# Pooled attention and a gated MLP on one core: left-over tokens stored token by token, two small vectors loaded late, half of a weight loaded through GpSimd's queue

## The chip, the cores and the metric

The kernel runs on one core of a Trainium2 chip. A time is the device time of one execution in microseconds (us); where several runs are given, their median counts. The engines are TensorE (PE in the profile; PEld is its weight load), VectorE (DVE), ScalarE (ACT), GpSimd (POOL) and SyncE (SP). SP computes nothing here; it issues DMAs.

## What is computed

```python
# B, H, S, D = 8, 8, 576, 64; keys and values are averaged over groups of 8 tokens: 72 of each
k_p = k.reshape(B, H, 72, 8, D).mean(axis=3);  v_p = v.reshape(B, H, 72, 8, D).mean(axis=3)
attn = softmax(q @ k_p.T / sqrt(D))              # 576 x 72 for each batch and head
x = (attn @ v_p), heads side by side             # [B, 576, 512]
h = gelu(x @ w_in)                               # w_in 512 x 1024
u, v = h[..., :512], h[..., 512:]
v_n = (v - mean) / sqrt(var + 1e-6) * g_ln       # over the 512 features
v_s = w_sg @ v_n + b_sg[:, None]                 # over the 576 tokens
out = x + (u * v_s) @ w_out
```

`w_in` and `w_out` arrive as 64-bit floats, and the kernel makes 32-bit floats of them with integer operations.

## The kernel before

**Steps and the written-out order.** The work of a batch is cut into steps named by a letter and a number: A and B load k and v, E loads the left-over tokens, C loads q, K pools the keys and writes the block matrix `kbd`, P pools the values, Q transposes q, S makes scores and softmax, L and T transpose the attention weights, V multiplies by the values (this gives x), H makes the value half of h and normalises it, U the other half, W multiplies by `w_sg` and gates, O multiplies by `w_out`, Z stores. Lower-case names are weights: `lv0`, `lv1` load the two pieces of w_in's value half, `lu0`, `lu1` those of its other half, `lo0`, `lo1` those of w_out, `ls0` loads w_sg; `v0` to `v3`, `u0` to `u3`, `o0` to `o3` and `s0` to `s4` convert or transpose one piece each. A step is a generator, and each time its name stands in a list it advances by one piece. `PROLOGUE` is that list for batch 0 and the beginning of batches 1 to 3, together with all the weights; `PERIOD` is run once for each later batch. `S0+1` is the first group of heads one batch later. Each engine issues its instructions in the order in which the lists emit them.

**Left-over tokens.** 72 pooled tokens of a head are 64, which have tiles of their own, and 8 left over. `load_left` brings the raw tokens of those 8 of all 8 heads into one tile `left`, four DMAs of 32 rows of 2 KB (lines 263 and 266): keys in partitions 96 to 127, values in 64 to 95. A row is a head and a token, and the tokens of a head stand together. The pooled rows `lp` (L315) are transposed with the pooled keys (L336, L338) and copied into `kbd` (L345, L346). The attention weights of left-over tokens are gathered by GpSimd into `el` (L465), transposed (step L), and split into `lt` (L476 or L479, L480 and L482), which step V multiplies by `vl`, the left-over values times `mask` (L381).

**Start.** GpSimd writes the constants, among them `mask` with a memset and two selects (L112 to L116). SP issues all loads, in the order of the list: all of them go through `load` (L155). In one queue at most eight of SP's DMAs are under way: the ninth waits for the first. b_sg, spread over 128 partitions as `bbc`, and g_ln as `gcol` are loaded with w_sg in `load_wsg`, and are first read in step W (L616).

**Conversion of w_in.** A piece is converted by two ACT instructions (L196, L197), two of DVE (L199, L200), one of POOL (L202), an ACT cast (L205) into `wih` and a POOL subtraction (L207) into `wil`.

**The row around the first V of batch 1.** The two halves of `lt` each need two ACT casts (L479, L480) and one DVE subtraction (L482); the last four normalised tiles of H (`vg`, L575) are cast to `vhh` or `vht` (L583), which step W multiplies.

Of the kernel before, what the change touches and what calls it, by code (L numbers as in the profile page):

```python
# [20 lines left out]


PROLOGUE = """
A1+0 A0+0 lv0 v1 E0+0 v1 K0+0 C0+0 v0 K0+0 K2+0 C1+0 K1+0 C2+0 Q0+0 K1+0 K2+0 Q1+0 v0 Q0+0 K2+0 C3+0 S0+0 v1 v0 lv1
Q2+0 v1 S0+0 B1+0 B0+0 Q3+0 Q1+0 v1 ls0 S1+0 v0 S1+0 Q2+0 S0+0 E0+1 S1+0 S0+0 S2+0 Q3+0 A0+1 v3 T0+0 S1+0 S2+0 S3+0
S0+0 v3 S3+0 S3+0 S2+0 P0+0 lu0 v0 S2+0 S3+0 v2 v3 S3+0 A1+1 P1+0 S1+0 S2+0 S3+0 P2+0 T0+0 s3 v3 T1+0 S3+0 S3+0 L0+0
s3 v3 v2 C0+1 v2 s4 s3 T1+0 K0+1 L0+0 s4 C1+1 V0+0 B0+1 v2 K2+1 lo0 T2+0 s4 s1 V0+0 s1 T2+0 u1 v2 V1+0 V1+0 V2+0 T3+0
s2 u1 V2+0 K1+1 V0+0 T3+0 K2+1 u0 lu1 K2+1 s2 s1 u1 V3+0 Q0+1 V3+0 u0 Q1+1 s2 V1+0 S0+1 S0+1 S0+1 S1+1 u1 V2+0 V1+0
V3+0 u0 S1+1 V2+0 S0+1 S1+1 u0 V0+0 H0+0 H2+0 u1 S1+1 S0+1 S0+1 H0+0 P0+1 S0+1 H2+0 S1+1 u3 s0 s0 V3+0 T0+1 H0+0 U1+0
H2+0 s0 U1+0 S1+1 H1+0 T0+1 u0 B1+1 H0+0 P1+1 C3+1 u3 P2+1 C2+1 H2+0 H0+0 S1+1 S0+1 Q2+1 u2 u2 H2+0 H0+0 Q3+1 H1+0  # L30
P2+1 T0+1 H4+0 P2+1 H4+0 u2 H4+0 S2+1 H3+0 H2+0 S3+1 S2+1 H4+0 S1+1 C1+2 S2+1 u2 u2 u3 C0+2 H1+0 H3+0 S2+1 U0+0 u3
S3+1 u3 S3+1 S2+1 H4+0 S3+1 H3+0 U0+0 P2+1 o0 H1+0 U2+0 H4+0 S3+1 S2+1 S3+1 S2+1 U3+0 S2+1 lo1 H1+0 S3+1 o1 A1+2 o1
U2+0 E0+2 H4+0 S3+1 H1+0 L0+1 H3+0 T1+1 H3+0 L0+1 H4+0 L0+1 H3+0 Q0+2 o1 U3+0 W2+0 L0+1 o1 V0+1 o1 o3 o0 T1+1 K1+2
W2+0 T1+1 o3 W3+0 T2+1 o0 o0 W3+0 o0 V0+1 o2 V1+1 o2 T2+1 o2 T2+1 W0+0 A0+2 V1+1 V2+1 o3 K0+2 o2 W2+0 V1+1 T3+1 B0+2
W1+0 K2+2 V2+1 W2+0 T3+1 W0+0 W0+0 T3+1 W3+0 o2 K2+2 K2+2 V3+1 C2+2 W0+0 W1+0 W3+0 P0+2 W1+0 W1+0 S0+2 O0+0 S0+2 V1+1
O1+0 Q2+2 V2+1 V3+1 S0+2 B1+2 A0+3 O0+0 P1+2 Q1+2 S0+2 V3+1 S1+2 O0+0 A1+3 O1+0 P2+2 o3 S1+2 S1+2 S2+2 O2+0 O1+0 S2+2
C3+2 V0+1 S2+2 Z0+0 O2+0 S1+2 o3 V3+1 Z0+0 H2+1 H2+1 Q3+2 C0+3 O2+0 Z1+0 S0+2 T0+2
""".split()
# [12 lines left out]
def tile_pooled_attn_gmlp(ctx: ExitStack, tc: tile.TileContext, q, k, v, w_in, g_ln, w_sg, b_sg, w_out, out):  # L51
    nc = tc.nc
# [170 lines left out]

# [93 lines left out]
    def step_K(b, i):  # L317
        if i < 2:
            if ("kp", b) not in st:
                st["kp", b] = per.tile([P, G, D], F32, name="kp")  # L320
# [12 lines left out]
        kp = st.pop(("kp", b))
        ps = atile()
        for a in range(2):
            nc.tensor.transpose(ps[:, 0, P * a:P * (a + 1)],  # L336
                                kp[:, 2 * a:2 * a + 2].rearrange("p h d -> p (h d)"), ident)
        nc.tensor.transpose(ps[:, 1, 0:P], lp.rearrange("p h d -> p (h d)"), ident)  # L338
# [4 lines left out]
        for h in range(2):
            r = slice(D * h, D * h + D)
            nc.scalar.mul(kbd[r, :, JL + JM * h:JL + JM * (h + 1)], main[r], c)  # L345
            nc.scalar.mul(kbd[r, :, LEFT[h]:LEFT[h] + JL], left[r], c)  # L346
# [69 lines left out]
    def step_S(b, g):  # L416
        qT = st.pop(("qT", b, g))
        flat = (mtile() if b == 0 else atile()).rearrange("p a n -> p (a n)")
        slots = []
# [9 lines left out]
        nc.vector.tensor_reduce(out=nmax, in_=every.rearrange("p s (h k) -> p s h k", h=2),  # L429
                                axis=AX.X, op=ALU.max, negate=True)  # L430
# [4 lines left out]
        mode = 2 if (b, g) in SOFTMAX else 0
        if mode == 2:

            scores = every.rearrange("p s (h k) -> p s h k", h=2)
            nc.vector.tensor_tensor(e, scores, nmax.unsqueeze(3).broadcast_to([P, NT, 2, SP]), op=ALU.add)
            yield  # L440
            nc.scalar.activation(e, e, AF.Exp)
        else:
            for i in range(NT):
                for h in range(2):
                    acc = {} if mode else {"accum_out": ssum[:, i, h:h + 1]}
                    nc.scalar.activation(e[:, i, h], slots[i][:, h], AF.Exp, bias=nmax[:, i, h:h + 1], **acc)  # L446
# [12 lines left out]
        nc.vector.tensor_tensor(e, e, rec.unsqueeze(3).broadcast_to([P, NT, 2, SP]), op=ALU.mult)  # L459
# [4 lines left out]
        for h in range(2):
            nc.gpsimd.tensor_copy(st["el", b][:, :, JL * (2 * g + h):JL * (2 * g + h + 1)],  # L465
                                  ef[:, :, LEFT[h]:LEFT[h] + JL])
# [277 lines left out]
```

## Times and profile before

| | |
|---|---|
| runs | 584.28 us median of 3 (583.62 to 584.38) |
| profiled execution | 584.24 us, of which the span of its instructions is 582.5 us |
| PE | 554.7 us busy, 95% of the span |
| PEld, DVE, ACT, POOL | 522.9, 405.6, 351.9, 222.7 us busy |
| DMA | 46.34 MB, of which 36.23 MB are read |
| granted TensorE clock | 0.991 |

Busy time is the union of an engine's recorded instructions; the matmuls' ends are modelled. "[idle before <-releaser]" behind a row is the time in which the engine had nothing running ahead of it, and what ended that time.

### The profile page before, as it was taken

The numbers are of one execution on the slowest core, as the hardware profiler recorded it, in microseconds if no ns is written. First come the engines' busy times: TensorE is split into PE (matmuls) and PEld (weight loads), VectorE is DVE, ScalarE is ACT, GpSimd is POOL, SyncE is SP. The second block draws the span as 40 slices with busy tenths as digits, with TensorE's granted clock in tenths as the row PEclk, the third lists the DMA queues.
The fourth block names the chain that finished last, engine by engine and source line by source line (L and its number), as shares of the span: only waits on it lengthen the run. The fifth ranks groups of instructions, "written<-read, shape, count | busy, mean of one in ns | idle before, by whom it ended". The sixth has DMA issues, their size and how long they took to land.

```text
span 582.5 us, 10319 instructions
## 1 busy us (share of the span) xinstructions
PE 554.7 (95%) x3793; PEld 522.9 (90%) x3793; DVE 405.6 (70%) x555; ACT 351.9 (60%) x1000; POOL 222.7 (38%) x301
## 2 busy tenths in 40 slices
PE   3698988999999999999999999999999999999995
PEld 3576788998999989999999989999999989998995
DVE  0579998988668795778667785688667765344434
ACT  2888776788547775497456765497456775412310
POOL 4365565833326131522416231532417131433230
PEclk9899998999999999999999999999999999999998
DMA  8988460462431634233441724134350211021105
GB/s 199 240 223 236 72 169 27 100 132 47 90 73 37 117 58 97 58 68 51 94 79 37 119 56 96 33 73 72 82 90 1 43 20 21 1 42 22 20 1 82
DMA packets 161282, 46.34 MB, mean 80 GB/s; under 512 B 148752, under 2 KB 148752, under 8 KB 161232
## 3 DMA queue, kind: packets, MB, share of 16 engines
q1 hardware_dynamic: 156464, 45.10, 37.9%
q10 hardware_dynamic: 4768, 0.59, 0.7%
q8 instruction: 30, 0.49, 0.4%
q14 instruction: 20, 0.16, 0.1%
HBM read 36.23 MB, written 9.44 MB: 78 GB/s over the span
## 4 chain that ended last, share of the span: by engine, by line
PE 79%; DVE 10%; ACT 4%; DMA 3%; SPq 2%; issue 1%; ACTq 0%; POOL 0%; DVEq 0%
PE mps L99 65%; PE aps L99 11%; PE aps L135 3%; ACT e L446 2%; SPq L155 2%; DMA left<-in_v 1%; DMA qraw<-in_q 1%; DVE e L459 1%; DVE bst L569 1%; DVE nmax L429 1%; DVE vg L575 1%; DVE vp L315 1%; DMA out<-y 1%; DVE ssum L449 1%; DVE qT L412 1%
## 5 line engine op out<-in xcount | busy, mean ns | idle before, releaser
L99 PE MATMUL mps<-xhl,wih 128*128 128x288 f32 x512 | 89.9, 298 | 0.0
L627 POOL TENSOR_TENSOR glo<-u,ghi 128x576 fp32r<-128x576 f32 x32 | 45.4, 1431 | 108.7 <-ACT ghi L625 106.8
L99 PE MATMUL mps<-wih,xhl 128*128 128x512 f32 x256 | 85.6, 400 | 0.1
L99 PEld LDWEIGHTS mps<-xhl,wih 128*128 128x128 f32 x512 | 75.8, 189 | 1.4
L446 ACT ACTIVATE e<-aps,nmax 128x72 f32<-128x72 f32 x240 | 73.4, 352 | 2.7 <-DVE nmax L429 2.4
L616 DVE SCALAR_TENSOR_TENSOR mps<-mps,gcol,bbc 128x576 f32<-128x576 f32 x32 | 26.4, 826 | 51.8 <-PE mps L99 51.7
L99 PEld LDWEIGHTS mps<-wih,xhl 128*128 128x128 f32 x256 | 48.1, 188 | 10.7 <-DVE x L659 0.3
L446 ACT ACTIVATION_READ_ACCUMULATOR e<-aps,nmax 128x1 f32 x240 | 57.1, 238 | 0.0
L99 PE MATMUL mps<-wsh,vhh 128*128 128x288 f32 x256 | 56.4, 302 | 0.0
L99 PE MATMUL mps<-wsl,vhh 128*128 128x288 f32 x256 | 55.4, 298 | 0.0
L99 PE MATMUL mps<-wsh,vhl 128*128 128x288 f32 x256 | 55.2, 297 | 0.0
L99 PE MATMUL mps<-xhl,wil 128*128 128x288 f32 x256 | 55.0, 296 | 0.0
L572 POOL TENSOR_TENSOR rstd<-mv,eps 128x1 f32<-128x1 f32 (+1 forms) x40 | 11.1, 277 | 114.0 <-DVE mv L570 104.5
L527 POOL TENSOR_TENSOR xhl<-x,xhl 128x576 fp32r<-128x576 f32 x32 | 45.3, 1430 | 23.9 <-ACT xhl L525 23.9
L575 DVE TENSOR_SCALAR vg<-vg,mv,rstd 128x512 f32<-128x512 f32 (+1 forms) x40 | 40.1, 1005 | 19.3 <-POOL rstd L573 19.3
L99 PE MATMUL mps<-ghi,woh 128*128 128x288 f32 x240 | 52.7, 301 | 0.0
L99 PE MATMUL mps<-ghi,wol 128*128 128x288 f32 x240 | 51.4, 295 | 0.0
L99 PE MATMUL mps<-glo,woh 128*128 128x288 f32 x240 | 51.4, 295 | 0.0
L99 PE MATMUL mps<-wil,xhl 128*128 128x512 f32 x128 | 50.6, 395 | 0.0
L565 ACT ACTIVATE vg<-mps 128x512 f32<-128x512 f32 x32 | 19.2, 599 | 45.4 <-PE mps L99 45.2
L585 POOL TENSOR_TENSOR vhl<-vg,vhh 128x512 fp32r<-128x512 f32 x32 | 42.2, 1319 | 9.4 <-ACT vhh L583 8.7
L625 ACT CAST ghi<-u 128x576 fp32r<-128x576 f32 x32 | 21.4, 673 | 39.5 <-DVE u L618 38.8
(158 smaller groups left out, 1423.9 us busy)
## 6 DMA issues: line engine op xcount, KB each, us to landing
out<-y SPq DMA_DIRECT2D x118, 72.0 KB
kvraw<-in_k SPq DMA_DIRECT2D x32, 256.0 KB
qraw<-in_q SPq DMA_DIRECT2D x112, 72.0 KB
kvraw<-in_v SPq DMA_DIRECT2D x28, 256.0 KB
raw<-in_moe_w_in SPq DMA_DIRECT2D x4, 1024.0 KB
raw<-in_moe_w_out SPq DMA_DIRECT2D x2, 1024.0 KB
stage<-in_moe_w_sg SPq DMA_DIRECT2D x4, 288.0 KB
left<-in_k SPq DMA_DIRECT2D x16, 64.0 KB
```

The lines of the kernel that those rows point to most:

```text
L99: nc.tensor.matmul(o, lhsT, rhs, start=start, stop=stop)
L135: nc.tensor.transpose(ps[:rows, i * P:(i + 1) * P], src(i), ident if i < NT - 1 else swap)
L155: queue.dma_start(o, i)
L446: nc.scalar.activation(e[:, i, h], slots[i][:, h], AF.Exp, bias=nmax[:, i, h:h + 1], **acc)
L527: (nc.vector if b in LO_DVE else nc.gpsimd).tensor_tensor(xhl[:, 1, g], x32[:, g], xhl[:, 0, g].bitcast(F32), op=ALU.subtract)
L565: nc.scalar.activation(vg, o, AF.Gelu_apprx_tanh)
L572: nc.gpsimd.tensor_tensor(rstd, mv[:, 1:2], eps[:n, 1:2], op=ALU.add)
L575: nc.vector.tensor_scalar(vg, vg, mv[:, 0:1], rstd, op0=ALU.subtract, op1=ALU.mult)
L585: (nc.gpsimd if i < NT - 1 else nc.vector).tensor_tensor(lo, vg, hi.bitcast(F32), op=ALU.subtract)
L616: nc.vector.scalar_tensor_tensor(vs, vs, gcol[:, d:d + 1], bbc.rearrange("p (a n) -> p a n", a=2), op0=ALU.mult, op1=ALU.add)
L625: nc.scalar.copy(ghi[:, d], uf)
L627: nc.gpsimd.tensor_tensor(glo[:, d], uf, ghi[:, d].bitcast(F32), op=ALU.subtract)
```

## The change

1. `load_left` orders the rows by token first and head second (`h j g (r d)` for k, `j h (r d)` for v). What reads the rows follows: `kbd`'s copy (`p (j g)`), the place that `el` is gathered to, now with a step of four elements between the tokens, and `mask`, which is now 1/8 where the row's index modulo 4 is the column.
2. `mask` is made by DVE from the identity, by one reduction and one multiplication, instead of by GpSimd.
3. b_sg and g_ln leave `load_wsg` and have a function and a name of their own, `lb0`, late in the prologue.
4. `W_POOL = ("v",)`: the two DMAs of w_in's value half are issued by GpSimd.
5. `PROLOGUE` is written in another order. It holds the same names as before, each as often, and `lb0`. `PERIOD` is as before.

```diff
-A1+0 A0+0 lv0 v1 E0+0 v1 K0+0 C0+0 v0 K0+0 K2+0 C1+0 K1+0 C2+0 Q0+0 K1+0 K2+0 Q1+0 v0 Q0+0 K2+0 C3+0 S0+0 v1 v0 lv1
+A0+0 A1+0 E0+0 C0+0 C1+0 lv0 K0+0 K2+0 K1+0 B0+0 Q0+0 Q0+0 K0+0 C2+0 K1+0 C3+0 Q1+0 lv1 K2+0 B1+0 Q1+0 ls0 A0+1 K2+0
...
-    W_POOL = ()
+    W_POOL = ("v",)
...
-    nc.gpsimd.memset(mask, 1.0 / POOL)
     sl = mask[64:96, :]
-    nc.gpsimd.affine_select(out=sl, in_=sl, compare_op=ALU.is_ge, fill=0.0, base=0,
-                            pattern=[[-JL, 4]], channel_multiplier=1)
-    nc.gpsimd.affine_select(out=sl, in_=sl, compare_op=ALU.is_ge, fill=0.0, base=JL - 1,
-                            pattern=[[JL, 4]], channel_multiplier=-1)
+    nc.vector.tensor_reduce(out=sl, in_=ident[64:96, 64:96].rearrange("p (j a) -> p a j", a=4), axis=AX.X, op=ALU.add)
+    nc.vector.tensor_scalar(sl, sl, 1.0 / POOL, None, op0=ALU.mult)
...
+
+    def load_vectors():
         load(bbc, b_sg.rearrange("(o t) -> o t", o=1).broadcast_to([P, S]))
         load(gcol, g_ln.rearrange("(c p) -> p c", p=P))
...
-        src = k[b].rearrange("(g h) (j r) d -> h g j (r d)", h=2, r=POOL)
+        src = k[b].rearrange("(g h) (j r) d -> h j g (r d)", h=2, r=POOL)
         for h in range(2):
-            load(t[96:P, h], src[h, :, JM:SP])
-        src = v[b].rearrange("h (j r) d -> h j (r d)", r=POOL)
+            load(t[96:P, h], src[h, JM:SP])
+        src = v[b].rearrange("h (j r) d -> j h (r d)", r=POOL)
         for gp in range(2):
-            load(t[64:96, gp], src[4 * gp:4 * gp + 4, JM:SP])
+            load(t[64:96, gp], src[JM:SP, 4 * gp:4 * gp + 4])
...
-        left = ps[:, 1, 96:P].rearrange("p (g j) -> p g j", g=G)
+        left = ps[:, 1, 96:P].rearrange("p (j g) -> p g j", g=G)
...
-            nc.gpsimd.tensor_copy(st["el", b][:, :, JL * (2 * g + h):JL * (2 * g + h + 1)],
+            nc.gpsimd.tensor_copy(st["el", b].rearrange("p t (n j a) -> p t n j a", n=2, a=4)[:, :, g // 2, :, 2 * (g % 2) + h],
                                   ef[:, :, LEFT[h]:LEFT[h] + JL])
...
+            elif name[1] == "b":
+                load_vectors()
```

How the new list moves instructions shows best at three places. The first is SP's beginning, before the change: k of batch 0, the first piece of w_in's value half, the left-over tokens, then q (`early` and `qraw` are both tiles of q; `early<-in_v` is v).

```order
L155 DMA kvraw<-in_k 64x2x512 x4
L155 DMA raw<-in_moe_w_in 128x2x1024
L155 DMA left<-in_k 32x1x512 x2
L155 DMA left<-in_v 32x1x512 x2
L155 DMA early<-in_q 96x6x64 x6
L155 DMA qraw<-in_q 96x6x64 x2
L155 DMA raw<-in_moe_w_in 128x2x1024
L155 DMA early<-in_v 64x2x512 x4
L155 DMA stage<-in_moe_w_sg 128x576 x4
L155 DMA stage<-in_moe_w_sg 64x576
L155 DMA bbc<-in_moe_b_sg 128x576
L155 DMA gcol<-in_moe_g_ln 128x4x1
```

SP's beginning after the change:

```order
L152 DMA kvraw<-in_k 64x2x512 x4
L152 DMA left<-in_k 32x1x512 x2
L152 DMA left<-in_v 32x1x512 x2
L152 DMA early<-in_q 96x6x64 x4
L152 DMA early<-in_v 64x2x512 x2
L152 DMA early<-in_q 96x6x64 x2
L152 DMA qraw<-in_q 96x6x64 x2
L152 DMA early<-in_v 64x2x512 x2
L152 DMA stage<-in_moe_w_sg 128x576 x4
L152 DMA stage<-in_moe_w_sg 64x576
L152 DMA kvraw<-in_k 64x2x512 x2
L152 DMA raw<-in_moe_w_in 128x4x512
```

Both pieces of w_in's value half and the two small vectors have left this stretch; k of batch 1 follows w_sg directly, where the vectors, the left-over tokens of batch 1 and then k stood. The two pieces are now issued by GpSimd, behind its last memset and ahead of its first conversion:

```order
L350 MEMSET vb 128x512
L352 MEMSET vl 64x512
L355 MEMSET lt 64x576 x2
L152 DMA raw<-in_moe_w_in 128x2x1024 x2
L199 TENSOR_TENSOR top<-top,raw 128x512 x2
L204 TENSOR_TENSOR wil<-top,wih 128x512 x2
```

The second place is ACT's beginning, before:

```order
L196 ACT_TABLE_LOAD
L196 ACTIVATE top<-raw 128x512
L197 ACTIVATE raw<-raw 128x512
L196 ACTIVATE top<-raw 128x512
L197 ACTIVATE raw<-raw 128x512
L326 COPY kp<-aps 128x128 x2
L408 COPY qT<-mps 128x576
L345 ACTIVATE kbd<-aps 64x4x64
L346 ACTIVATE kbd<-aps 64x4x8
L345 ACTIVATE kbd<-aps 64x4x64
L346 ACTIVATE kbd<-aps 64x4x8
L205 CAST wih<-top 128x512
```

ACT's beginning after:

```order
L407 COPY qT<-mps 128x576
L325 COPY kp<-aps 128x128 x2
L407 COPY qT<-mps 128x576
L344 ACTIVATE kbd<-aps 64x4x64
L345 ACTIVATE kbd<-aps 64x4x8
L344 ACTIVATE kbd<-aps 64x4x64
L345 ACTIVATE kbd<-aps 64x4x8
L193 ACTIVATE top<-raw 128x512
L194 ACTIVATE raw<-raw 128x512
L193 ACTIVATE top<-raw 128x512
L194 ACTIVATE raw<-raw 128x512
L445 ACTIVATE e,ssum<-mps,nmax 128x72 x10
```

The first two conversions of w_in (four instructions) stood ahead of everything else and now stand between `kbd` and the first exponentials, and the second copy of q (`qT`) stands ahead of `kbd`. On PE, likewise, both first groups of q are now transposed ahead of the pooled keys. The third place is DVE ahead of the first V of batch 1, before:

```order
L459 TENSOR_TENSOR e<-e,aps 128x720
L199 TENSOR_SCALAR top<-top 128x512
L200 SCALAR_TENSOR_TENSOR top<-raw,top 128x512
L575 TENSOR_SCALAR vg<-vg,mv,rstd 128x512
L585 TENSOR_TENSOR vht<-vg,vht 64x512
L482 TENSOR_TENSOR lt<-aps,lt 32x576
L412 STREAM_TRANSPOSE qT<-qraw 128x576
L482 TENSOR_TENSOR lt<-aps,lt 32x576
```

The same stretch of DVE after:

```order
L458 TENSOR_TENSOR e<-e,aps 128x720
L574 TENSOR_SCALAR vg<-vg,mv,rstd 64x512
L196 TENSOR_SCALAR top<-top 128x512
L197 SCALAR_TENSOR_TENSOR top<-raw,top 128x512
L574 TENSOR_SCALAR vg<-vg,mv,rstd 128x512
L196 TENSOR_SCALAR top<-top 128x512
L197 SCALAR_TENSOR_TENSOR top<-raw,top 128x512
L481 TENSOR_TENSOR lt<-aps,lt 32x576
L584 TENSOR_TENSOR vht<-vg,vht 64x512
L481 TENSOR_TENSOR lt<-aps,lt 32x576
```

The 64-row `vg` has come down into this stretch, a second conversion pair stands ahead of the first `lt`, `vht` has moved between the two `lt`, and the transpose of q has moved behind them. On ACT the two casts for the first `lt` now stand ahead of the last cast of `vhh` instead of behind it.

More of the change, by code (lines that the diff above doesn't have):

```diff
@@ L23 @@
 PROLOGUE = """
-A1+0 A0+0 lv0 v1 E0+0 v1 K0+0 C0+0 v0 K0+0 K2+0 C1+0 K1+0 C2+0 Q0+0 K1+0 K2+0 Q1+0 v0 Q0+0 K2+0 C3+0 S0+0 v1 v0 lv1
[L25 to L37, printed above, removed]
+A0+0 A1+0 E0+0 C0+0 C1+0 lv0 K0+0 K2+0 K1+0 B0+0 Q0+0 Q0+0 K0+0 C2+0 K1+0 C3+0 Q1+0 lv1 K2+0 B1+0 Q1+0 ls0 A0+1 K2+0
@@ new lines @@
+v0 lu0 S0+0 S1+0 S0+0 Q2+0 Q3+0 v0 v1 S0+0 v1 v1 S1+0 Q2+0 v1 S0+0 E0+1 v0 S1+0 v0 C1+1 v1 A1+1 Q3+0 S1+0 v0 v3 S2+0
+S2+0 S1+0 T0+0 S3+0 v3 S2+0 S3+0 S0+0 v3 P1+0 S3+0 S3+0 v2 S2+0 S2+0 T0+0 v3 S3+0 S3+0 P0+0 S3+0 P2+0 C0+1 S3+0 s3
+T1+0 v3 T1+0 s4 s3 K0+1 v2 L0+0 lo0 L0+0 V0+0 s4 s4 V0+0 u1 s3 K2+1 T2+0 V1+0 T2+0 s1 u1 T3+0 K1+1 v2 V1+0 B0+1 V2+0
+v2 Q0+1 T3+0 s2 v2 Q1+1 s1 V2+0 K2+1 V3+0 K2+1 V0+0 S0+1 u0 V3+0 s1 u0 S0+1 S0+1 s2 u1 S1+1 S1+1 u1 S0+1 s2 V1+0 C3+1
+S1+1 V3+0 V2+0 u0 V0+0 S0+1 S0+1 Q3+1 V2+0 S1+1 C2+1 lu1 S0+1 H2+0 H2+0 H0+0 S1+1 T0+1 V1+0 s0 P0+1 B1+1 u1 H0+0 lb0
@@ new lines @@
+s0 T0+1 A0+2 S1+1 U1+0 s0 H2+0 u0 H0+0 u3 u0 T0+1 U1+0 H2+0 H2+0 S1+1 Q2+1 H1+0 V3+0 S0+1 u3 P1+1 S3+1 S3+1 u2 H4+0
+H1+0 H0+0 S1+1 H2+0 u3 u3 P2+1 P2+1 u2 H4+0 H0+0 P2+1 H0+0 u2 H4+0 H3+0 S3+1 S2+1 H4+0 H1+0 S2+1 H3+0 S3+1 S2+1 H1+0
+C0+2 U0+0 u3 H3+0 S2+1 S3+1 U3+0 lo1 S2+1 u2 U0+0 u2 A1+2 S2+1 H4+0 S3+1 H1+0 H1+0 P2+1 S2+1 S3+1 o0 S2+1 U3+0 H4+0
+o1 H4+0 S3+1 U2+0 C1+2 L0+1 o1 T1+1 L0+1 H3+0 H3+0 o0 L0+1 H4+0 H3+0 o1 W2+0 L0+1 U2+0 V0+1 K1+2 T1+1 o0 o0 Q1+2 o0
+o1 V0+1 W3+0 o2 T1+1 V1+1 T2+1 T2+1 o1 K0+2 W2+0 W0+0 B1+2 o2 T2+1 E0+2 Q0+2 V1+1 o2 V2+1 o3 T3+1 o3 o2 W3+0 V1+1
@@ L38 @@
+T3+1 V2+1 W0+0 K2+2 o3 W0+0 W1+0 W2+0 W0+0 T3+1 K2+2 W3+0 C2+2 o2 V3+1 K2+2 S0+2 W1+0 P1+2 V3+1 W1+0 W2+0 B0+2 S1+2
+S0+2 W1+0 S0+2 P0+2 o3 W3+0 P2+2 O1+0 O1+0 o3 Q2+2 S0+2 S0+2 A1+3 O0+0 C3+2 V0+1 O1+0 S1+2 V3+1 O0+0 S2+2 O0+0 S2+2
+O2+0 V2+1 Q3+2 S1+2 Z0+0 O2+0 O2+0 S2+2 A0+3 Z0+0 Z1+0 C0+3 H2+1 S1+2 V1+1 H2+1 V3+1 T0+2
 """.split()
```

## The prediction

> **What bounds the kernel now.** I read the page first: PE is busy nearly all the span.
>
> ```profile
> span 582.5 us, 10319 instructions
> ```
>
> The share of busy time says nothing of where the rest is lost, so next I read the busy time of each engine by stretches of the span. The columns are the stretch and its length, then busy us and count for PE, PEld, DVE, ACT and POOL, the granted clock, the DMA share and GB/s.
>
> ```profile
> 0.00:10.00 10.00, 1.82 (x8) 1.85 (x9) 0.00 (x0) 1.28 (x1) 5.93 (x24) 1.00 0.75 215
> 10.00:20.00 10.00, 8.03 (x63) 7.43 (x62) 4.93 (x6) 6.27 (x15) 3.72 (x3) 1.00 0.94 209
> 20.00:30.00 10.00, 6.31 (x39) 5.74 (x37) 5.49 (x11) 9.32 (x52) 1.67 (x4) 0.83 1.05 249
> 30.00:40.00 10.00, 8.94 (x65) 7.51 (x64) 6.76 (x11) 9.57 (x28) 6.56 (x11) 1.00 0.80 213
> 40.00:50.00 10.00, 8.75 (x44) 6.35 (x43) 9.70 (x9) 8.45 (x17) 6.46 (x5) 1.00 0.87 176
> 100.00:120.00 20.00, 20.00 (x152) 19.70 (x152) 18.67 (x20) 14.77 (x42) 15.77 (x12) 1.00 0.44 100
> ```
>
> From 100 us PE is busy 20.00 us of 20.00: there it sets the pace, and whatever arrives there earlier or later moves the end by as much. Up to 40 us the DMA share is 0.75 to 1.05, and from 20 us ACT is busy over 9 of 10. From 40 us DVE is (9.70 of 10). So the prologue is limited by transfers, then ACT, then DVE, and the change can pay only there. The chain of waits names where DVE hands over to PE, and the waits of DVE between 40 and 140 us say where that chain has slack:
>
> ```profile
> 93.50 1.68 PE aps L99 x8
> DVE kp L315 <- DMA kvraw<-in_k: 2.7, 1, 2.7
> DVE lt L482 <- ACT lt L480: 1.7, 2, 1.1
> ```
>
> At 93.50 PE starts V of batch 1, and from there it hardly waits. Ahead of it DVE waits once 2.7 us for k of batch 1 and twice, 1.7 us together, for `lt`. When that V starts is what I forecast; the rest of the program follows it.
>
> **The start, up to the last softmax of batch 0.** The DMA issues, with KB each:
>
> ```profile
> kvraw<-in_k SPq DMA_DIRECT2D x32, 256.0 KB
> raw<-in_moe_w_in SPq DMA_DIRECT2D x4, 1024.0 KB
> left<-in_k SPq DMA_DIRECT2D x16, 64.0 KB
> left<-in_v SPq DMA_DIRECT2D x16, 64.0 KB
> early<-in_q SPq DMA_DIRECT2D x6, 144.0 KB
> bbc<-in_moe_b_sg SPq DMA_DIRECT2D x1, 288.0 KB
> ```
>
> And the rows of the timeline on the way to the first scores and through ACT's stretch:
>
> ```profile
> 8.18 5.77 PE L99 MATMUL aps<-kvraw,ident 128*128 128x128 f32 x32 [8.18 <-DMA kvraw<-in_k]
> 11.92 0.67 ACT L196 ACTIVATE top<-raw 128x512 f32<-128x512 f32 x1 [9.84 <-DMA raw<-in_moe_w_in]
> 15.83 0.39 PE L336 MATMUL aps<-ident,kp 128*128 128x128 f32 x2
> 16.37 0.30 PE L338 MATMUL aps<-ident,lp 128*128 128x128 f32 x1 [0.16 <-DVE lp L315]
> 16.56 0.69 PE L405 MATMUL mps<-ident,early 96*128 96x96 f32 x6
> 16.71 0.38 ACT L345 ACTIVATE kbd<-aps 64x256 f32<-64x256 f32 x1
> 17.46 0.18 ACT L346 ACTIVATE kbd<-aps 64x32 f32<-64x32 f32 x1
> 19.78 0.64 ACT L408 COPY qT<-aps 128x576 f32<-128x576 f32 x1 [0.28 <-PE aps L405]
> 28.82 0.32 ACT L446 ACTIVATE e<-mps,nmax 128x72 f32<-128x72 f32 x1 [0.68 <-DVE nmax L429]
> 34.84 0.91 DVE L459 TENSOR_TENSOR e<-e,mps 128x720 f32<-128x720 f32 x1
> ```
>
> The second group of q is transposed at 16.56. Ahead of it went k (4 x 256 KB), one piece of w_in (1024), `left` (4 x 64) and two groups of q (4 x 144): 2880 KB. After the change both have to be there as well before ACT can go on, since w_in's conversion stands ahead of the exponentials: the same 2880 KB, only through two queues. So I take the second group's transpose at 16.56 + x, with x near 0. Below it is bounded by PE: 8.18 + 5.77 = 13.95, and one group of 0.69 first, so 14.64, x = -1.9. Above, if both pieces of w_in go ahead of q, 1024 KB more (1.05 MB) at the mean of the first four stretches, 221.5 GB/s, take 4.7 us; since w_in's second piece can begin only behind its first, and q already has some in the rings, I take three quarters of it, x = +3.5 (an estimate from these rows).
>
> By the new order PE transposes that group ahead of the pooled keys: 0.69 + 0.39 + 0.30, then `kbd` takes 16.71 to 17.64, 0.93. `kbd` is done 2.3 us behind 16.56 + x, where it was 1.1 behind it: 1.2 later. ACT then converts w_in (4 x 0.67 = 2.68), which it did before in an idle stretch of 9.84 us; one copy of q (0.64) has moved ahead, and waits of 0.28 and 0.68 are covered by the conversions: 1.1 later. So the end of batch 0's softmax on DVE, 34.84 + 0.91 = 35.75, comes at 38.05 + x.
>
> The rule against GpSimd's queue is in the Trainium skill, DMA: Bandwidth & Descriptors, Rules for kernel authors: spreading DMAs over several issuing engines brings no bandwidth, since all run on the same 16 DMA engines. By it x would be 0 and no less, and the sum below would lose its better half of the first gain. No run so far shows two load queues at once.
>
> **Batch 1's keys on DVE.**
>
> ```profile
> 35.66 0.42 DVE L199 TENSOR_SCALAR top<-top 128x512 int32<-128x512 int32 x1
> 36.77 0.74 DVE L160 TENSOR_TENSOR wsl<-mps,wsh 128x576 fp32r<-128x576 f32 x1
> 40.19 1.98 DVE L315 TENSOR_REDUCE kp<-kvraw 128x128 f32<-128x1024 f32 x1 [2.67 <-DMA kvraw<-in_k]
> ```
>
> Before, DVE converted a piece and subtracted (35.66 to 37.51, 1.85 us), then waited 2.67 for k. After, `kp` comes first and those 1.85 behind it, so `kp` at 40.19 - 1.85 = 38.34 would be no change. Two things must be there. The softmax: 38.05 + x. And k: `bbc` (288 KB) and batch 1's `left` (4 x 64) no longer go ahead of it, 544 KB, 2.5 us at 221.5 GB/s: 37.7. The later decides: a lead of 0.3 at x = 0 and of 0.6 from x = -0.4 downwards. I take 0.5; if k came even sooner, x = -1.9 would give 2.2.
>
> `left` may also move faster. The Trainium skill, the same page, Why a DMA increments its semaphore by 16 and not by 1, says that a DMA runs on as many engines as divide its slowest dimension: by that 4 heads gave four, 8 tokens give eight. No row here shows the engines of one DMA, and nothing of the sum rests on it.
>
> **The hand-over to PE.** The rows of DVE and ACT there:
>
> ```profile
> 82.16 1.02 DVE L575 TENSOR_SCALAR vg<-vg,mv,rstd 128x512 f32<-128x512 f32 x2
> 85.23 0.90 DVE L459 TENSOR_TENSOR e<-e,aps 128x720 f32<-128x720 f32 x1
> 87.17 1.50 DVE L575 TENSOR_SCALAR vg<-vg,mv,rstd 128x512 f32<-128x512 f32 x1
> 88.70 0.69 DVE L585 TENSOR_TENSOR vht<-vg,vht 64x512 fp32r<-64x512 f32 x1
> 92.61 0.75 DVE L482 TENSOR_TENSOR lt<-aps,lt 32x576 fp32r<-32x576 f32 x1 [0.53 <-ACT lt L480]
> 102.44 0.42 DVE L199 TENSOR_SCALAR top<-top 128x512 int32<-128x512 int32 x1
> 102.89 0.69 DVE L200 SCALAR_TENSOR_TENSOR top<-raw,top 128x512 int32<-128x512 int32 x1
> 88.70 0.62 ACT L583 CAST vhh<-vg 128x512 fp32r<-128x512 f32 x1 [3.05 <-DVE vg L575]
> 91.31 0.63 ACT L479 CAST lt<-aps 32x576 fp32r<-32x576 f32 x1 [0.81 <-DVE lt L482]
> 91.38 0.43 PE L99 MATMUL mps<-wtl,vht 128*128 128x288 f32 x2
> ```
>
> Before, ACT waited 3.05 us for `vg` with the casts for `lt` behind that wait, and DVE then waited for them. From the end of the last `e` (85.23 + 0.90 = 86.13) to that of the second `lt` (93.36) it took 7.23. After, the first `lt`'s casts do not stand behind `vhh`, and DVE has conversions to do meanwhile. The 64-row `vg` (1.02 / 2 = 0.51) has moved behind that point, which is so reached at 85.62. Then come 0.51, a pair (0.42 + 0.69 = 1.11), a `vg`, another pair of 1.11, `lt` 0.75, `vht` 0.69, `lt` 0.75; the second `lt` needs two casts (2 x 0.63) behind the first, of which `vht` covers 0.69, so 0.57 are added. With `vg` at 0.51 or at the 1.50 it took here this is 6.0 or 7.0: the end at 91.6 or 92.6 instead of 93.36. Gain 0.75 to 1.75; I take the middle, 1.2. What is late next is W, whose last matmuls ended at 91.81: more than 1.7 us needs W to come sooner too.
>
> **Edits at nothing.** `mask` on DVE: two small instructions in its idle first 10 us (0.00 busy above). GpSimd's DMA issues: behind them stands a conversion that waits for DVE and for these very DMAs. `bbc` and `gcol` late: behind them in SP's order is batch 2, and their first reader stands behind the second `lt`; without that cover DVE would wait in step W. Gathering `el` with a step: GpSimd, from nothing to twice its time,
>
> ```profile
> L465 POOL COPY el<-e 128x40 f32<-128x40 f32 x64 | 12.4, 226 | 52.3 <-ACT vg L565 27.7 <-DVE e L459 24.5
> ```
>
> 226 ns each; PE waits for the last two of a batch, so up to 0.45 us once in the prologue. I take 0, the copy being no larger. In the periods PE sets the pace and nothing of this counts.
>
> **Sum.** 0.5 + 1.2 = 1.7 us off the profiled execution's 584.24 (its span 582.5 and 1.74 around it; 0.04 from the median of the runs, 584.28): 582.5.
>
> **Rivals.** *q starved by the second queue (slower).* Place: the rings, 8 to 18 us. q moves in runs of 64 floats, w_in in runs of 1024; if the DMA engines take turns between the queues run by run, q gets the small share until w_in is through. Price: with x = 3.5 the softmax ends at 41.55, 3.2 behind 38.34; less 1.2 that is 2.0 slower, 586.2. It decides from x = 1.5, the transpose at 18.1. For it: 256-byte runs against 4 KB. Against: the first stretches' DMA share of 0.75 to 0.94 leaves room. The Trainium skill, DMA: Bandwidth & Descriptors, Queues, rings and completion order, has the engines turn from queue to queue by packets, which is the rule that would make this so. Chance 0.18. *The transfer saved is not saved (same).* k lands at 40.19 as before, with 1.85 us still to do: 1.85 - 1.2 = 0.65 slower, 584.9, within what can be told from no change (0.2%, 1.2 us). Chance 0.17. *More.* Two queues fill the rings better, x = -1.9 and k with it, and the 1.50 `vg` shrinks: 2.2 + 1.7 = 3.9, 580.3. For it: the low rates of 209 to 215 GB/s. Chance 0.10. My forecast has 0.55, about a seventh of it within 0.2%.
>
> So faster 0.57, same 0.25, slower 0.18. The range goes from "more" at 580.3 to 585.6, into the starved case, with one in ten left out at each side.
>
> **What would show it.** Right: the second group's transpose by 16.6, `kp` of batch 1 near 37.8, no DVE wait at the `lt`, V of batch 1 near 91.8. Wrong: that transpose after 18, ACT waiting for w_in's first piece behind `kbd`, or PE idle between 100 and 140 us.

## The result, and the profile after

The changed kernel takes 587.06 us (median of 9 runs, 586.14 to 590.34), beside 584.28 (9 runs) for the kernel before on the same chip: a ratio of 1.0061, 95% interval 1.0045 to 1.0076. It is slower, 1.5 us outside the forecast range. The profiled execution took 588.31 against 584.24, and 4.0 of these 4.07 us lie in its span, 586.5 us for 582.5. It is one of the longer of the nine runs: the medians differ by 2.8 us, so what the timelines explain is the larger 4.07.

First the busy time by stretches, with the columns of the prediction:

```profile
0.00:10.00 10.00, 4.29 (x21) 4.33 (x22) 2.01 (x3) 1.28 (x1) 6.97 (x23) 1.00 0.71 189
10.00:20.00 10.00, 3.39 (x24) 2.97 (x24) 1.47 (x1) 0.98 (x3) 0.00 (x0) 0.83 1.13 281
20.00:30.00 10.00, 7.05 (x38) 6.47 (x36) 4.80 (x9) 8.03 (x31) 1.80 (x2) 0.66 1.12 262
30.00:40.00 10.00, 9.10 (x51) 8.74 (x52) 6.42 (x12) 9.12 (x46) 5.41 (x8) 0.66 0.87 222
```

Between 10 and 20 us every engine does far less than before (PE is busy 3.39 us for 8.03, DVE 1.47 for 4.93, ACT 0.98 for 6.27) while the DMA engines move more than before (281 GB/s for 209). So bytes flow, and they are the wrong ones. The granted clock, which was 1.00, 0.83 and 1.00 in the three stretches from 10 to 40 us, is 0.83, 0.66 and 0.66. The timeline of PE says for what it waited:

```profile
5.71 5.72 PE L99 MATMUL aps<-kvraw,ident 128*128 128x128 f32 x32 [5.71 <-DMA kvraw<-in_k]
17.05 1.20 PE L404 MATMUL mps<-ident,early 96*128 96x96 f32 x6 [5.62 <-DMA early<-in_q]
19.23 1.20 PE L404 MATMUL mps<-ident,early 96*128 96x96 f32 x6 [0.98 <-DMA early<-in_q]
22.08 5.00 PE L99 MATMUL mps<-kbd,qT 128*128 128x144 f32 x20 [1.02 <-ACT kbd L345]
```

k is pooled at 5.71 instead of 8.18. In both kernels PE begins with the half of k that step A0 loads. The old list loads it behind the other half (A1, A0), the new list ahead of it (A0, A1). It is not w_in that moved away: the old list with w_in on GpSimd's queue, run below, still begins at 7.80. But then PE waits 5.62 us for q. The second group's transpose starts at 19.23, where 16.56 + x was forecast: x = 2.67. It takes 1.20 us instead of 0.69: the clock is already down, at 0.50 between 17 and 26 us. The two DMA queues between 9 and 11 us (packets, MB, time as a share of the engines'; q0 is GpSimd's, with w_in, q1 is SP's, with q):

```profile
q0 software_dynamic: 181, 0.74, 92.3%
q1 hardware_dynamic: 175, 0.04, 10.2%
```

The counts fit one packet of each in turn: 175 against 181, and 180 against 171 between 12 and 14 us. But q's packet is one run of 256 bytes and w_in's is 4 KB, and so q gets 0.04 MB of 0.78. The timeline of DVE shows what this came to:

```profile
41.93 0.90 DVE L458 TENSOR_TENSOR e<-e,mps 128x720 f32<-128x720 f32 x1
42.75 1.95 DVE L314 TENSOR_REDUCE kp<-kvraw 128x128 f32<-128x1024 f32 x1
47.07 0.75 DVE L236 TENSOR_TENSOR wtl<-mps,wth 64x576 fp32r<-64x576 f32 x1 [1.31 <-ACT wth L234]
90.76 0.90 DVE L458 TENSOR_TENSOR e<-e,aps 128x720 f32<-128x720 f32 x1
94.79 0.75 DVE L481 TENSOR_TENSOR lt<-aps,lt 32x576 fp32r<-32x576 f32 x1
97.31 0.75 DVE L481 TENSOR_TENSOR lt<-aps,lt 32x576 fp32r<-32x576 f32 x1
```

The softmax ends at 42.83 (35.75 before), `kp` begins at 42.75 (no-change point 38.34), neither `lt` waits any more, and the second ends at 98.06 instead of 93.36. The 4.70 us come apart so:

| stretch | before | after | difference |
|---|---|---|---|
| to `kp`, from its no-change point | 38.34 | 42.75 | +4.41 |
| from there to the end of the last `e` | 47.79 | 48.91 | +1.12 |
| from there to the end of the second `lt` | 7.23 | 6.40 | -0.83 |

### The profile page after: what moved, and what is told of

It reads as the page before. It is cut to its first block, busy times and chain, and to the rows that moved or that the text cites. A ratio compares the mean times of both kernels' runs of the same rounds, so it can differ in the third digit from the quotient of the medians.

```text
span 586.5 us, 10314 instructions
## 1 busy us (share of the span) xinstructions
PE 558.1 (95%) x3793; PEld 526.0 (90%) x3793; DVE 407.8 (70%) x557; ACT 352.0 (60%) x1000; POOL 225.7 (38%) x300
## 4 chain that ended last, share of the span: by engine, by line
PE 82%; DVE 8%; DMA 3%; ACT 2%; issue 2%; SPq 2%; POOL 1%; DVEq 0%; ACTq 0%
PE mps L99 66%; PE aps L99 11%; PE aps L132 4%; DMA early<-in_q 2%; SPq L152 2%; DVE nmax L428 1%; DVE e L438 1%; DVE ssum L448 1%; DVE vp L314 1%; DMA kvraw<-in_k 1%; DVE kp L314 1%; DMA kvraw<-in_v 1%; ACT e L445 1%; DVE qT L411 0%; DVE e L458 0%
## 5 line engine op out<-in xcount | busy, mean ns | idle before, releaser
L624 ACT CAST ghi<-u 128x576 fp32r<-128x576 f32 x32 | 21.3, 672 | 37.7 <-DVE u L617 37.7
```

What stands on the lines that cost most here:

```text
L624: nc.scalar.copy(ghi[:, d], uf)
```

## The experiments

Theory 1: w_in on GpSimd's queue holds q back. Theory 2, its main rival: the new order or the layout is what costs, and the queue is harmless. Theory 3: beside the late data, the clock that falls behind the idle PE has a price of its own. Times are medians; ratios are to the kernel before on the same chip, where the changed kernel has 1.0061.

**w_in back on SP's queue**, the rest as in the changed kernel:

```diff
-    W_POOL = ("v",)
+    W_POOL = ()
```

> The changed kernel with one part undone: w_in's value half goes through SP's queue again, at the places that the new list gives it (the first piece behind the second group of q). Theory 1 (GpSimd's queue holds q back): the second group of q is transposed before 15 us instead of at 19.2, batch 0's softmax ends some 5 us sooner than in the changed kernel, and the time is 582 to 584 us, 3 to 5 below the changed kernel's. Theory 2 (the new list costs the time, with the conversions of w_in between kbd and the exponentials): the second group may come sooner, but ACT then waits for w_in's first piece, and the time stays at 586 to 588.

581.01 us, ratio 0.9949 [0.9930, 0.9968]. PE and DVE in its timeline:

```profile
11.48 1.41 PE L404 MATMUL mps<-ident,early 96*128 96x96 f32 x12
21.15 1.22 PE L404 MATMUL aps<-ident,early 96*128 96x96 f32 x6 [3.76 <-DMA early<-in_q]
36.99 1.95 DVE L314 TENSOR_REDUCE kp<-kvraw 128x128 f32<-128x1024 f32 x1
91.56 0.75 DVE L481 TENSOR_TENSOR lt<-aps,lt 32x576 fp32r<-32x576 f32 x1
```

Both groups of q are transposed from 11.48, without a wait, and everything to the second `lt` comes 5.75 us sooner than in the changed kernel. The gain is a little larger than I had put it (582 to 584 us). That one word costs 1.1%, and the rest of the change is faster than before. Theory 2 falls.

**The queue alone**, in the kernel before:

```diff
-    W_POOL = ()
+    W_POOL = ("v",)
```

> The kernel before with GpSimd's queue alone (old list, old layout, early vectors). Theory 1 (the queue holds q back): the second group of q is transposed at 18 to 20 us instead of 16.6, the first scores start 1.5 to 3 us later than at 17.7, and the time is 585.5 to 587.5. Theory 2 (the list): no slower than before, 583.5 to 584.5, or faster, since the first piece of w_in no longer goes ahead of the left-over tokens in SP's queue.

590.39 us, ratio 1.0095 [1.0068, 1.0122]: the direction of theory 1, but dearer than I had put it. ACT and PE in its timeline:

```profile
15.95 0.66 ACT L196 ACTIVATE top<-raw 128x512 f32<-128x512 f32 x1 [13.86 <-DMA raw<-in_moe_w_in]
18.47 0.69 PE L336 MATMUL aps<-ident,kp 128*128 128x128 f32 x2 [4.88 <-ACT kp L326]
```

In the old order ACT's copies of the pooled keys stand behind w_in's first conversion, and that now waits for w_in's first piece until 15.95 (11.92 before, when it stood right behind k in SP's queue). PE waits 4.88 us for the copies. So what is late here is w_in, not q: the first group of q is transposed at 12.93, sooner than the 15.31 of before, and the second at 20.14 behind the late copies. The run confirms that the queue costs, but not that it is q that pays.

**The old order with the rest of the change**: layout, `mask`, late vectors; w_in on SP's queue. Of the list its one line with `lb0` is shown, the others being those of before.

```diff
-    W_POOL = ("v",)
+    W_POOL = ()
...
-S1+1 V3+0 V2+0 u0 V0+0 S0+1 S0+1 Q3+1 V2+0 S1+1 C2+1 lu1 S0+1 H2+0 H2+0 H0+0 S1+1 T0+1 V1+0 s0 P0+1 B1+1 u1 H0+0 lb0
+V3+0 u0 S1+1 V2+0 S0+1 S1+1 u0 V0+0 H0+0 H2+0 u1 S1+1 S0+1 S0+1 H0+0 P0+1 S0+1 H2+0 S1+1 u3 s0 s0 V3+0 T0+1 lb0 H0+0 U1+0
```

> The changed kernel with the old list and SP's queue: the layout by tokens, mask on DVE and the two vectors late (lb0 put in behind the first T0+1) are left of the change. Theory 1: k of batch 1 is there about 2.5 us sooner, so that DVE's wait of 2.7 us for it shrinks to under 1, and the time is 581.5 to 583. Theory 2 (these parts cost time, through the strided gather of el or the reading of kbd's left-over columns): 584.5 to 586.

582.51 us, ratio 0.9978 [0.9960, 0.9996], as theory 1 has it. DVE:

```profile
38.09 1.94 DVE L314 TENSOR_REDUCE kp<-kvraw 128x128 f32<-128x1024 f32 x1
89.62 0.75 DVE L481 TENSOR_TENSOR lt<-aps,lt 32x576 fp32r<-32x576 f32 x1 [1.14 <-ACT lt L479]
91.70 0.75 DVE L481 TENSOR_TENSOR lt<-aps,lt 32x576 fp32r<-32x576 f32 x1 [0.53 <-ACT lt L479]
```

`kp` no longer waits for k, and the two waits at `lt` are still there: it is the new order that removes those.

**PE kept busy**: the changed kernel, with identity matmuls (into columns that nothing reads) ahead of the first two groups' transposes.

```diff
+            for i in range((18, 5, 0, 0)[g]):
+                mm(ps[:, 1, 384:512], ident, ident, True, True)
```

> The changed kernel with 18 matmuls of the identity ahead of the first group of q and 5 ahead of the second, whose results nobody reads: PE is kept busy while it waits for q. Theory 3 (the idle stretch of PE costs more than its length, because a lower clock is granted behind it: 0.50 from 17 to 27 us, where ten score matmuls took 2.5 us instead of 1.4): the clock stays at 1.00 up to 25 us, the scores take 1.5 us for ten, and the time is 1 to 2.5 us below the changed kernel's, 584.5 to 586. If the clock falls as before, or the time stays at 586.5 to 588, the lower clock is not due to that idle stretch or costs nothing.

584.57 us, ratio 1.0021 [0.9997, 1.0046], 0.4% below the changed kernel. PE in its timeline:

```profile
10.92 4.18 PE L99 MATMUL mps<-ident 128*128 128x128 f32 x36
17.21 0.69 PE L406 MATMUL mps<-ident,early 96*128 96x96 f32 x6 [2.11 <-DMA early<-in_q]
19.06 0.69 PE L406 MATMUL mps<-ident,early 96*128 96x96 f32 x6
21.30 2.72 PE L99 MATMUL mps<-kbd,qT 128*128 128x144 f32 x20 [1.23 <-ACT kbd L345]
```

And its third stretch, with the columns of the result's first table of stretches:

```profile
20.00:30.00 10.00, 5.19 (x42) 4.81 (x42) 5.50 (x9) 9.82 (x45) 3.75 (x3) 0.99 1.15 244
```

And DVE, the last row of batch 0's softmax:

```profile
40.02 0.90 DVE L460 TENSOR_TENSOR e<-e,mps 128x720 f32<-128x720 f32 x1
```

q arrives nearly as late as in the changed kernel (19.06 for 19.23), but at a clock of 0.99 the same 20 matmuls take 2.72 us instead of 5.00. The softmax ends at 40.92 instead of 42.83, 1.91 us sooner, of which 0.17 are q's. The medians give 2.3 us; their two intervals just touch, so it is the timeline that decides. Theory 3 holds beside theory 1.

**Shorter runs on GpSimd's queue**: each piece of w_in in four loads of a quarter of its columns.

```diff
-        load(raw, sv, nc.gpsimd if name in W_POOL else nc.sync)
+        if name in W_POOL:
+            for f in range(4):
+                load(raw[:, :, 256 * f:256 * f + 256], sv[:, :, 256 * f:256 * f + 256], nc.gpsimd)
+        else:
+            load(raw, sv)
```

> The changed kernel, with each piece of w_in cut into four loads of a quarter of its columns, so that GpSimd's queue moves runs of 1 KB instead of 4 KB. Theory 1 (the DMA engines take turns packet by packet): per turn q gets 256 bytes against 1 KB, a share of 0.2 instead of 0.06, so that the 576 KB of two groups of q need no more than w_in's own 2 MB ahead of them: between 10 and 12 us q moves 0.12 to 0.25 MB instead of 0.07, the second group is transposed at 16 to 17.5 instead of 19.23, and the time is 583.5 to 586. Rival (GpSimd's queue is served first, whatever its packets): q moves 0.07 MB or less while w_in has packets queued, the transpose stays at 18.7 to 20, the time at 586 to 588. Under both w_in's second piece begins later, since GpSimd issues eight loads instead of two.

585.54 us, ratio 1.0023 [1.0012, 1.0035], within what theory 1 gave, but not for its reason. The queues between 8 and 12 us:

```profile
q0 software_dynamic: 167, 0.55, 56.7%
q1 hardware_dynamic: 1581, 0.43, 52.8%
```

GpSimd's issues, and the second group on PE:

```profile
6.05 2.37 POOL L152 DMA_DIRECT2D raw<-in_moe_w_in  x3
11.38 0.73 POOL L152 DMA_DIRECT2D raw<-in_moe_w_in  x1 [2.96 <-issue]
15.37 0.69 PE L408 MATMUL mps<-ident,early 96*128 96x96 f32 x6 [1.64 <-DMA early<-in_q]
```

The packets of w_in hardly got shorter: 0.55 MB in 167 are 3.3 KB each, so several runs went in one. What changed is that GpSimd issued three loads and then stood still before the fourth, so that 0.55 MB of w_in moved in these four us, where the changed kernel moved 1.17, and q had the engines between. It says that a slower second queue lets q through, nothing on the length of runs.

**The second piece of w_in later**: `lv1` moved behind the third step of w_in's second conversion.

```diff
-C2+0 K1+0 C3+0 Q1+0 lv1 K2+0 B1+0
+C2+0 K1+0 C3+0 Q1+0 K2+0 B1+0
...
-S0+0 v1 v1 S1+0 Q2+0
+S0+0 v1 v1 lv1 S1+0 Q2+0
```

> The changed kernel, with w_in's second piece issued by GpSimd only behind its addition in the second conversion, some 10 us later; the first piece is where it was. Theory 1: only 1 MB stands beside q, it is through by 12.3 us, and q follows at the full rate: the second group is transposed at 14 to 15.5 instead of 19.23, and the time is 582 to 584.5, behind the kernel with all of w_in on SP's queue only by what the first piece holds q back. Rival (a load on GpSimd's queue costs by itself, by its descriptors or its waits on GpSimd): 586 to 588 as in the changed kernel.

592.18 us, ratio 1.0137 [1.0112, 1.0162]: a miss in time. PE, GpSimd and ACT:

```profile
15.68 0.69 PE L404 MATMUL mps<-ident,early 96*128 96x96 f32 x6 [1.11 <-DMA early<-in_q]
25.35 0.71 POOL L152 DMA_DIRECT2D raw<-in_moe_w_in  x1
37.19 0.66 ACT L193 ACTIVATE top<-raw 128x512 f32<-128x512 f32 x1 [7.05 <-DMA raw<-in_moe_w_in]
```

With one piece beside it q comes 3.55 us sooner (15.68), as theory 1 said, if a little later than the 14 to 15.5 I had put. But the second piece, issued at 25.35, was there only at 37.19, 11.8 us later, and ACT waited 7.05 us for it. I had taken it to land as fast as those of the changed kernel, whose median the page gives:

```profile
raw<-in_moe_w_in POOLq DMA_DIRECT2D x2, 1024.0 KB, 7.8
```

The trace shows where the time went. Between 25 and 31 us GpSimd's queue moved no packet at all, and SP's queue kept the engines busy; the piece itself moved between 31 and 35 us:

```profile
q0 software_dynamic: 263, 1.04, 64.6%
```

So at least 5.6 of the 11.8 us lie ahead of its first packet, where the changed kernel's first packets of w_in moved within 2 us of their issue. If queues take turns, packets that were ready would have had some before, which speaks for something on GpSimd's side; what it was is not shown.

**Exponentials ahead of w_in's conversion**: the kernel of the first experiment, with batch 0's first exponentials moved up.

```diff
-v0 lu0 S0+0 S1+0 S0+0 Q2+0 Q3+0 v0 v1 S0+0 v1 v1 S1+0
+lu0 S0+0 S1+0 S0+0 S0+0 v0 Q2+0 Q3+0 v0 v1 v1 v1 S1+0
```

> The changed kernel with w_in on SP's queue, and the exponentials of batch 0's first group put ahead of w_in's first conversions, which made ACT wait 3.63 us for w_in's first piece with those exponentials behind it. If ACT sets the end of batch 0's softmax there, it comes 1 to 2 us sooner and the time is 579.5 to 580.5. Rival (batch 1's k, or w_in's conversion on DVE and GpSimd, is what comes last there): the same 581.0 as without this, within 0.5.

582.62 us, ratio 0.9973 [0.9956, 0.9989]: no gain, rather a loss of 0.2%. DVE:

```profile
21.78 0.43 DVE L196 TENSOR_SCALAR top<-top 128x512 int32<-128x512 int32 x1 [3.75 <-ACT top L193]
38.36 1.96 DVE L314 TENSOR_REDUCE kp<-kvraw 128x128 f32<-128x1024 f32 x1
```

DVE now waits 3.75 us for the conversion in place of the exponentials, and `kp` comes at 38.36 instead of 36.99. The start itself came 0.9 us later in this run too, so the size of the loss is not settled.

**Left-over tokens head by head again**, on top of the first experiment; `kbd`'s copy, `el` and `mask` go with it.

```diff
-        src = k[b].rearrange("(g h) (j r) d -> h j g (r d)", h=2, r=POOL)
+        src = k[b].rearrange("(g h) (j r) d -> h g j (r d)", h=2, r=POOL)
...
-        src = v[b].rearrange("h (j r) d -> j h (r d)", r=POOL)
+        src = v[b].rearrange("h (j r) d -> h j (r d)", r=POOL)
```

> The changed kernel with w_in on SP's queue, and the left-over tokens laid out head by head as before; of the change only the order of issue and the late vectors are left. If the layout pays by itself (left lands sooner, on more DMA engines), this is 0.5 to 1.5 us slower than the same kernel with the layout token by token, 581.5 to 582.5. Rival (the layout is worth nothing here, since left lands ahead of k's last piece in any case): 581.0, within 0.5.

580.77 us, ratio 0.9939 [0.9922, 0.9956], which overlaps the 0.9949 of the layout token by token: the layout pays nothing that can be told here. DVE:

```profile
34.80 1.95 DVE L314 TENSOR_REDUCE kp<-kvraw 128x128 f32<-128x1024 f32 x1
89.27 0.75 DVE L481 TENSOR_TENSOR lt<-aps,lt 32x576 fp32r<-32x576 f32 x1
```

`kp` is 3.54 us ahead of its no-change point, and the second `lt` ends 3.34 sooner than before. The order of issue with the late vectors, and with `mask` made by DVE, which no run undoes, is all of the gain.

**Longer runs of q beside GpSimd's queue**: six neighbouring tokens to a partition, runs of 1536 bytes.

```diff
-                load(t[:, :, h], q[b, 2 * g + h].rearrange("(t p) d -> p t d", t=6))
+                load(t[:, h], q[b, 2 * g + h].rearrange("(p t) d -> p t d", t=6))
...
+            for h in range(2):
+                for w in range(2):
+                    nc.scalar.copy(qT[64 * h:64 * h + 64].rearrange("p (n t w) -> p w t n", t=3, w=2)[:, w],
+                                   ps[64 * w:64 * w + 64, h, 0:HALF].rearrange("p (t n) -> p t n", t=3))
```

> The changed kernel, with q of batch 0 loaded six neighbouring tokens to a partition, so that q moves in runs of 1536 bytes instead of 256 beside w_in's 4 KB on GpSimd's queue, which issues as in the changed kernel. ACT pays for it with four copies of 64 partitions to a group (about 0.4 us each by the 64x256 rows) instead of one of 0.64. Theory 1 (turns by packets, so that q's share goes with the length of its runs): q moves at least 0.2 MB between 10 and 12 us instead of 0.07, and the second group is transposed at 14.5 to 17 instead of 19.23; the time is 583 to 586, the better start less up to 2 us of copies. Rival (GpSimd's queue is served first): transposed at 18.5 or later, and 587 to 590.

592.50 us, ratio 1.0149 [1.0131, 1.0166]. The queues between 12 and 15 us:

```profile
q0 software_dynamic: 198, 0.81, 77.3%
q1 hardware_dynamic: 196, 0.25, 24.9%
```

PE with the second group's last half, and ACT:

```profile
17.40 0.74 PE L405 MATMUL mps<-ident,early 96*128 96x96 f32 x3 [1.00 <-DMA early<-in_q]
18.18 2.67 ACT L410 COPY qT<-mps 64x288 f32<-64x288 f32 x4 [0.32 <-PE mps L405]
```

Again one packet each, 196 against 198, and with packets six times as long q's share is 0.24 of the bytes instead of 0.05. That is theory 1's rule, and the rival, that GpSimd's queue goes first, does not fit it. q is there 1.83 us sooner, still later than I had put it: between 9 and 11 us SP's queue sent almost nothing,

```profile
q0 software_dynamic: 190, 0.78, 97.4%
q1 hardware_dynamic: 17, 0.02, 3.2%
```

though it had issued all four loads of the two groups by 9.01 us. Why q's next load did not move there stays open; turns alone do not explain it. The time was a miss, 6.5 us above my range: the copies take 2.67 us to a group instead of 0.64, four times, 8.1 us together.

**Longer runs of q without a second queue**: the same edit in the fastest kernel so far, head by head and with w_in on SP's queue.

> Left-over tokens head by head, w_in on SP's queue, the new order and the late vectors (580.8 as it was), and q of batch 0 in runs of 1536 bytes. If short runs cost by themselves, with no second queue beside them, the groups of q come sooner and the third and fourth no longer make PE wait 1.35 and 0.96 us: 579.5 to 581, the copies taking back part. Rival (the 256-byte runs cost nothing without a competing queue): 581 to 582.5, the copies alone.

589.21 us, ratio 1.0090 [1.0073, 1.0107]. PE's second group and ACT:

```profile
12.94 1.07 PE L405 MATMUL mps<-ident,early 96*128 96x96 f32 x6 [0.18 <-DMA early<-in_q]
12.80 2.69 ACT L410 COPY qT<-mps 64x288 f32<-64x288 f32 x4 [10.79 <-PE mps L405]
```

The second group of q comes no sooner than with short runs (12.94; there both groups are transposed within 1.46 us from 12.04), so the rival was right on that; for the third and fourth group the run does not show it, since PE came to them only at 24.0 us. The time was a miss under both: the edit costs 1.51%, 8.8 us, about the 8.1 by which the copies are longer. In the changed kernel the same edit cost 0.88%, 5.1 us. If the copies cost the same there, the 3.7 between are what longer runs give where a second queue stands beside them.

**The late vectors alone**, in the kernel before.

```diff
-S1+1 u3 s0 s0 V3+0 T0+1 H0+0 U1+0
+S1+1 u3 s0 s0 V3+0 T0+1 lb0 H0+0 U1+0
...
+            elif name[1] == "b":
+                load_vectors()
```

> The kernel before, with nothing changed but that b_sg and g_ln are loaded behind batch 1's first T. If the 288 KB ahead of batch 1's k made DVE wait, the 2.67 us wait at kp goes and the time is 582 to 583, as in the kernel with the layout and the late vectors. Rival (that wait is handed on to the waits at lt, or it was the layout that paid): within 0.5 of before.

583.37 us, ratio 0.9998 [0.9983, 1.0014]: nothing that can be told, so the rival. DVE:

```profile
38.82 1.97 DVE L317 TENSOR_REDUCE kp<-kvraw 128x128 f32<-128x1024 f32 x1 [1.64 <-DMA kvraw<-in_k]
```

The wait for k shrinks from 2.67 to 1.64 us and does not go. Whether the old order with layout and vectors (0.9978) is better than the vectors alone, two intervals that overlap do not say.

**PE kept busy in the fastest kernel**: 8 and 10 identity matmuls ahead of the third and fourth group.

```diff
+            for i in range((0, 0, 8, 10)[g]):
+                mm(ps[:, 1, 384:512], ident, ident, True, True)
```

> The fastest kernel so far (the new order, late vectors, left-over tokens head by head, w_in on SP's queue: 580.8), with 8 and 10 identity matmuls ahead of the transposes of batch 0's third and fourth group of q, where PE idled and the granted clock fell to 0.66 between 20 and 30 us. If a low clock costs wherever it falls, as the 2.5 us that such matmuls brought back in the changed kernel suggest: 578.5 to 579.8. Rival (only PE on the path pays; here ACT is busy 9.92 of 10 us between 20 and 30 and sets the pace, and DVE waits for PE's scores only 0.64): 580.2 to 581.2, though the clock rises to 0.8 or more.

580.22 us, ratio 0.9912 [0.9885, 0.9939], overlapping the 0.9939 without them. Its third stretch:

```profile
20.00:30.00 10.00, 8.21 (x71) 7.85 (x72) 6.80 (x12) 9.91 (x52) 6.66 (x9) 1.00 1.05 290
```

And DVE, the end of the softmax and `kp`, with the end of the softmax in the kernel without the matmuls as the last row:

```profile
33.78 0.91 DVE L460 TENSOR_TENSOR e<-e,mps 128x720 f32<-128x720 f32 x1
34.88 1.95 DVE L314 TENSOR_REDUCE kp<-kvraw 128x128 f32<-128x1024 f32 x1 [0.19 <-DMA kvraw<-in_k]
33.98 0.90 DVE L458 TENSOR_TENSOR e<-e,mps 128x720 f32<-128x720 f32 x1
```

The clock rises from 0.66 to 1.00, but the softmax ends only 0.19 us sooner (34.69 for 34.88), and `kp` stays where it was (34.80), now held for 0.19 us by k. That is the rival: a faster PE gains next to nothing there. ACT, 9.91 us of 10 busy, would explain it, but no run shows by itself that ACT sets the pace, and the intervals leave room for a gain of some tenths of a per cent. This and the kernel without the matmuls are the best versions, both faster than before and after.

## Why the prediction was wrong

**The failed step** is "the same 2880 KB, only through two queues", and with it "x near 0". It counted the bytes that have to be there and took it that they come in any order that helps. Here the two queues did not share bytes; they alternated packets (175 to 181, and 196 to 198 with longer runs), so that w_in's two pieces went ahead of q, though they were needed after it. x was 2.67. The rival of the starved q had the mechanism, the place and the rule in the Trainium skill (DMA: Bandwidth & Descriptors, Queues, rings and completion order: the engines turn from queue to queue by packets), with which the trace agrees. I gave it 0.18, since the DMA share of 0.75 to 0.94 "leaves room". That was the wrong row: a mean share says nothing of who gets the next turn. The lengths of the runs, which stood in the same paragraph, did.

**Its price was short.** At x = 2.67 the rival's own sum gives 40.72 for the end of the softmax, 1.2 slower in the end: 585.4. The softmax ended at 42.83. The missing 2.11 us were not priced by anybody: PE, idle for 5.62 us, came back at half the clock. With PE kept busy the softmax ends 1.91 us sooner, 1.74 of it not due to q, so the clock is most of the 2.11; the last 0.4 or so has no run of its own. The Trainium skill has a rule for this (TensorE: Matmul & The Clock Gate, Part 1: after an idle window of about 3.4 us PE runs at half rate). The runs agree in part: the clock fell in waits of 5.62 and 3.76 us and not behind one of 2.11. But in the changed kernel it fell a second time, at about 30.2 us, in a shorter one:

```profile
30.85 2.74 PE L99 MATMUL mps<-kbd,qT 128*128 128x144 f32 x10 [2.77 <-DVE e L458]
```

And in the kernel head by head it fell at about 21.5 us, where the waits of PE just before had been 1.35 and 0.96. So the length of one wait does not decide it here, and no run shows what does.

**The bound below, x = -1.9**, failed as well. It came from k's pooling at 8.18, with the old order of k's two halves; in the new order that starts at 5.71. With w_in behind q on SP's queue the second group is transposed 0.7 us into the row at 11.48, at 12.2, x = -4.4. So "more" was larger than I let it be.

**Batch 1's keys.** A lead of 0.3 to 0.6 was forecast, limited by the softmax at 38.05 and by k at 37.7. Both were too late: without the second queue `kp` ran at 36.99 and 34.80, 1.35 and 3.54 us ahead of the no-change point, the softmax done and k there.

**The hand-over** was right in kind and at its lower end in size: 0.83 for 0.75 to 1.75, and 0.83 and 0.91 in the two kernels without the second queue. Within it `vg` came out at its shorter value, 0.54, and `vht` took 1.71 instead of 0.69, which left the casts for the second `lt` nothing to add. Both waits at `lt` went, and only with the new order.

**Not seen**: 1.12 us between `kp` and the last `e`, the same in three kernels with the new order (48.91, 48.92, 48.90 for 47.79). A wait of 1.31 us of DVE for `wth` stands in it that the old order did not have.

**Edits at nothing**: the layout was worth nothing, as priced (0.9949 and 0.9939); so were `el`'s step, which goes with it, and the late vectors by themselves (0.9998). `mask` was not run by itself. Layout, `mask` and vectors together in the old order gave 0.9978 [0.9960, 0.9996], a gain just clear of none that no run puts down to one of them.

So of the change, the queue costs 1.1%, and the new order with late vectors and `mask` on DVE gains 0.6%.

## What to carry to other kernels

When a load is moved to a second queue, compare the lengths of the runs on both: if the engines alternate packets, as they did here, a queue of 4 KB packets takes sixteen times the bytes of one with 256-byte packets (0.74 MB against 0.04 in two us here), and what is needed first must not be the short one. Leave loads that are needed in an order on one queue in that order. And when an edit makes PE wait for some microseconds, price its slow return as well where the next step waits for PE; where it did not, in the last run, a full clock brought nothing that can be told.
